# Diagonal state blocks in the ring of ScalarE's copied sums, one sigmoid and SyncE's branch hint placed elsewhere

## Chip, cores and metric

One core of a Trainium2 chip runs the whole program. The metric is the device time in microseconds (us), the median of three runs. The engines are named as the profile names them: PE (TensorE's matmuls, with PEld for its weight loads), DVE (VectorE), ACT (ScalarE), POOL (GpSimd) and SP (SyncE, which here only issues transfers). A "q" after the name (ACTq, SPq) means the engine's sequencer: it waits, branches or issues a DMA while the engine itself does nothing.

## What is computed

A gated linear recurrence runs over 768 steps for 4 batches and 8 heads of 48 channels, and its output goes through a SwiGLU block (384 to 1536 to 384), all in fp32:

```python
f = 1.0 / (1.0 + np.exp(-f_logit))
for t in range(S):
    state = f[:, :, t, :, None] * state + np.einsum('bhd,bhe->bhde', k[:, :, t], v[:, :, t])
    y[:, :, t] = np.einsum('bhd,bhde->bhe', q[:, :, t], state)
x = y.transpose(0, 2, 1, 3).reshape(B * S, H * D)
g = x @ w_gate
out = (g * (1.0 / (1.0 + np.exp(-g))) * (x @ w_val)) @ w_out
```

## The kernel before

**Chunks and stages.** The sequence is cut into six chunks (c = 0 to 5) of 128 steps. In a chunk each of the four batches (b = 0 to 3) is one unit of attention. `attention(u)` is a generator whose steps are laid by hand between other work: the sigmoid of the gates (L580 from the third chunk on), transposes and scans on DVE, scores on PE (L647), `decay` (the state times the chunk's decay), the outputs `y` (L683 to L708), and the new state (L737). When a chunk's attention is done, its 512 tokens go through the SwiGLU block while the next chunk's attention runs beside it. From the second chunk on, that block (`mlp_fifteen`) computes four groups of fifteen products (L988), whose results ScalarE copies out of PSUM or DVE combines, and then seven products of the down projection (`down_seven`, L1087 and L1150).

**The order.** `times(c)` gives each step of each batch a place on a time line, and `come_in` calls the steps due before each product. `in_order` then fixes each engine's order to the order in which the program was written. An instruction that waits on ACT therefore holds everything written after it on ACT.

**Outputs of the attention.** For b = 0 to 2 of a later chunk, `y` is copied by ScalarE into the tile `yT` (L691, tag `"x"`, one buffer in the pool `att`), and ten small DMAs carry it from there into `xT`, the input of the SwiGLU block. From the third chunk on POOL issues them (L698). For b = 3 no copy through `yT` is needed: the states are laid out as a block diagonal matrix, `diagonal`, so that PE writes `y` directly in the layout of `xT` (L708), and ScalarE copies it there (L723). `decay` builds `diagonal`: ScalarE fills it with zeros (L568) and copies the two halves of the decayed states in (L570). Its tile has the tag `"x"` too. It is the same single buffer as `yT`, so L568 waits until the ten DMAs of b = 2 have read it.

**ScalarE's copied sums.** `aside` (L997) copies a product out of PSUM into a ring of three tiles with the tag `"aside"` in the pool `comb` (128 x 512 fp32 each); DVE adds or subtracts it soon after. Each group of fifteen products uses the ring six times.

**The down projection's banks.** In `down_seven`, step `two` ends with ScalarE's copy of a product into the output tile (L1113, `ob`). That product lies in the one PSUM bank with the tag `"B"`, and step `four` (`o5`, the matmuls `o<-ws,hs`) takes the same bank.

**The chunk's end.** `put_out` (L1096) sends half of a chunk's outputs from ACT's queue and the other half from POOL's (SP's in the last chunk). The sigmoid of chunk 3, batch 1 is placed by the list `sigmoid` in `times` (L872), 4 units ahead of the end of chunk 1's block of products, which is on the time line the place ahead of `seven`.

**The branch.** A second, general program (`general_path`) follows, for gates too small for the short way. A flag decides: `judge` computes it in the last chunk, all five engines load it (L1355), get a branch hint (L1357, `mark_branch_hint_location("redo", 0, ...)`), and branch at L1361. With these inputs the general program is skipped, so each engine jumps to the end of its instruction stream. There SP waits for the transfers that are still out, and all engines meet.

**Completion semaphores.** SP's and ACT's transfers share eight completion semaphores, handed out in turn. A transfer that is given one waits until the transfer that had it before has landed.

## Time and profile before

| | us |
|---|---|
| three runs | 608.42, 608.66, 609.53 |
| median | 608.66 |
| the profiled execution, whole | 609.78 |
| its span, first to last instruction | 608.0 |
| granted TensorE clock in it | 0.999 |

| engine | busy us | share of the span | instructions |
|---|---|---|---|
| PE | 592.7 | 97% | 4028 |
| DVE | 476.9 | 78% | 825 |
| ACT | 292.7 | 48% | 557 |
| POOL | 70.1 | 12% | 175 |

The profile is one execution. What lies around its span (609.78 less 608.0, 1.8 us) is launch and finish. A line of a timeline or of the chain of waits gives start in us, duration in us, engine, operation, and in square brackets the idle time before it with what ended it. In a list of waits the three numbers are the sum, the count and the longest. In a list of operations of one line the three durations are least, median and greatest in ns, followed by the first and the last start. Matmuls are pipelined, so those of one group start closer together than they last: the 24 matmuls of a 128x192 half step take 3.9 us from the first start to the next group's start.

### The profile page before, as it was taken

The numbers are of one execution on the slowest core, as the hardware profiler recorded it, in microseconds if no ns is written. First come the engines' busy times: TensorE is split into PE (matmuls) and PEld (weight loads), VectorE is DVE, ScalarE is ACT, GpSimd is POOL, SyncE is SP. The second block draws the span as 40 slices with busy tenths as digits, with TensorE's granted clock in tenths as the row PEclk, the third lists the DMA queues.
The fourth block names the chain that finished last, engine by engine and source line by source line (L and its number), as shares of the span: only waits on it lengthen the run. The fifth ranks groups of instructions, "written<-read, shape, count | busy, mean of one in ns | idle before, by whom it ended". The sixth has DMA issues, their size and how long they took to land.

```text
span 608.0 us, 10812 instructions
## 1 busy us (share of the span) xinstructions
PE 592.7 (97%) x4028; PEld 487.8 (80%) x4028; DVE 476.9 (78%) x825; ACT 292.7 (48%) x557; POOL 70.1 (12%) x175
## 2 busy tenths in 40 slices
PE   7899999999999999999999999999999999999996
PEld 5744555667888899878899888898988899988896
DVE  7999885968999977988895978994878981666731
ACT  3567662314776512476622476732276731366600
POOL 1000000000030150030330030330030321000000
PEclk9999999999999999999999999999999999999999
DMA  9999461014331145333344333253241100100001
GB/s 202 236 246 357 140 196 27 8 33 130 79 92 48 37 113 129 93 96 96 77 111 122 91 101 95 62 135 85 74 105 52 28 8 8 53 1 1 1 1 56
DMA packets 110300, 55.12 MB, mean 91 GB/s; under 512 B 72992, under 2 KB 102688, under 8 KB 110240
## 3 DMA queue, kind: packets, MB, share of 16 engines
q1 hardware_dynamic: 103872, 47.67, 30.0%
q0 software_dynamic: 4352, 3.94, 2.0%
q10 hardware_dynamic: 2016, 2.75, 1.2%
q8 instruction: 33, 0.54, 0.4%
q14 instruction: 27, 0.22, 0.1%
HBM read 44.56 MB, written 6.82 MB: 85 GB/s over the span
## 4 chain that ended last, share of the span: by engine, by line
PE 84%; DVE 10%; DMA 2%; issue 1%; ACT 1%; POOL 1%; SPq 0%; ACTq 0%; DVEq 0%; POOLq 0%
PE o L1087 17%; PE A L988 15%; PE B L988 12%; PE gate L786 5%; PE val L786 5%; PE c L988 5%; PE o L988 5%; PE sc L647 4%; PE o L1150 3%; PE o L809 3%; PE y L708 2%; PE y L687 2%; PE dS L728 1%; PE y L683 1%; DVE c L892 1%
## 5 line engine op out<-in xcount | busy, mean ns | idle before, releaser
L698 POOL DMA_DIRECT2D xT<-yT x120 | 59.9, 507 | 53.8 <-ACT yT L691 52.2
L988 PE MATMUL A<-xs,w_both 128*128 128x256 f32 x240 | 62.3, 382 | 1.0 <-ACT c L993 1.0
L1087 PE MATMUL o<-w_out,h 128*128 128x192 f32 x360 | 62.0, 327 | 0.5 <-DVE h L940 0.5
L1087 PEld LDWEIGHTS o<-w_out,h 128*128 128x128 f32 x360 | 58.7, 190 | 1.7 <-DVE h L940 0.8
L993 ACT COPY c<-A 128x512 f32<-128x512 f32 x40 | 23.3, 582 | 58.9 <-PE A L988 48.9
L988 PEld LDWEIGHTS A<-xs,w_both 128*128 128x128 f32 x240 | 44.8, 190 | 7.9 <-ACT c L993 1.4
L993 ACT COPY aside<-A 128x512 f32<-128x512 f32 x60 | 35.0, 584 | 33.1 <-PE A L988 33.0
L889 DVE TENSOR_TENSOR c<-c,aside 128x512 f32<-128x512 f32 x60 | 41.1, 686 | 12.1 <-ACT aside L993 10.4
L940 DVE TENSOR_TENSOR h<-h,c 128x256 f32<-128x256 f32 x100 | 40.5, 414 | 7.8 <-ACT h L1004 7.6
L662 DVE TENSOR_TENSOR A<-sc,causal 128x512 f32<-128x512 f32 x48 | 30.9, 685 | 17.2 <-PE sc L647 17.1
L892 DVE TENSOR_TENSOR c<-c,aside 128x512 f32<-128x512 f32 x60 | 41.0, 683 | 2.5 <-ACT aside L993 2.5
L1004 ACT ACTIVATE h<-c 128x256 f32<-128x256 f32 x100 | 39.2, 416 | 7.8 <-DVE c L889 5.6
L1087 PE MATMUL o<-ws,h 128*128 128x192 f32 x240 | 41.5, 328 | 0.2 <-DVE A L662 0.2
L988 PE MATMUL B<-xs,w_both 128*128 128x256 f32 x160 | 41.3, 380 | 0.1
L988 PE MATMUL A<-xs,extra 128*128 128x256 f32 x160 | 41.3, 380 | 0.0
L988 PE MATMUL c<-xT,w_both 128*128 128x256 f32 x160 | 41.2, 380 | 0.1
L988 PE MATMUL B<-xT,extra 128*128 128x256 f32 x160 | 41.1, 379 | 0.0
L635 POOL MEMSET gates<- 128x4 f32 x24 | 2.9, 122 | 327.9 <-DVE qT L559 322.8
L993 ACT COPY aside<-B 128x512 f32<-128x512 f32 x60 | 35.1, 584 | 9.7 <-PE B L988 6.7
L1087 PEld LDWEIGHTS o<-ws,h 128*128 128x128 f32 x240 | 39.1, 190 | 0.8 <-DVE A L662 0.4
L889 DVE TENSOR_TENSOR c<-c,o 128x384 f32<-128x384 f32 x15 | 8.3, 552 | 36.8 <-PE o L1087 36.8
L892 DVE TENSOR_TENSOR c<-o,c 128x512 f32<-128x512 f32 x40 | 27.4, 684 | 10.6 <-ACT h L1004 6.2
(142 smaller groups left out, 1199.9 us busy)
## 6 DMA issues: line engine op xcount, KB each, us to landing
fsquares<-in_f_logit_dram SPq DMA_DIRECT2D x64, 96.0 KB, 2.5
qsquares<-in_q_dram SPq DMA_DIRECT2D x64, 96.0 KB, 2.2
ksquares<-in_k_dram SPq DMA_DIRECT2D x64, 96.0 KB, 2.3
v<-in_v_dram SPq DMA_DIRECT2D x24, 192.0 KB, 2.9
w<-in_moe_w_gate_dram SPq DMA_DIRECT2D x6, 768.0 KB, 6.5
w<-in_moe_w_val_dram SPq DMA_DIRECT2D x6, 768.0 KB, 5.4
w<-in_moe_w_out_dram SPq DMA_DIRECT2D x6, 768.0 KB, 4.6
out_dram<-ob ACTq DMA_DIRECT2D x14, 192.0 KB, 2.5
```

Of the source, the lines that this page charges most:

```text
L647: nc.tensor.matmul(sc[par][:, a * C:(a + 1) * C], lhsT=kT[r, a, :], rhs=qT[r, a, :], start=True, stop=True)
L662: nc.vector.tensor_tensor(A[:, par], sc[par].rearrange("p (a t) -> p a t", t=C), causal.unsqueeze(1).broadcast_to((128, HP, C)), ALU.mult)
L698: (nc.gpsimd if c >= SQUARES else nc.sync).dma_start(out=xT[c][f % 128:f % 128 + n, f // 128, b * C:(b + 1) * C], in_=yT[r:r + n, par, a / ...
L786: nc.tensor.matmul(p, lhsT=w[:, j, i, :], rhs=xT[c][:, i, :], start=(i == 0), stop=(i == KT - 1))
L809: nc.tensor.matmul(p, lhsT=hidden_tile(h, n // 2)[:, n % 2 * 2 + b // 2, b % 2 * C:(b % 2 + 1) * C], rhs=w_out[:, j, :], start=(n == 0), s ...
L889: nc.vector.tensor_tensor(dst, a, b, ALU.add)
L892: nc.vector.tensor_tensor(dst, a, b, ALU.subtract)
L940: lagging.append(lambda: f(*args))
L988: nc.tensor.matmul(p[name][:, n, :], lhsT=weights_of[a][:, n, j, :], rhs=tokens[b], start=fresh and n == 0, stop=True, skip_group_check=True)
L993: nc.scalar.copy(t, p[name])
L1004: nc.scalar.activation(dst, src[:, 0, :], AF.Silu)
L1087: nc.tensor.matmul(p[:, n, :], lhsT=lhsTs[j][:, n * C:(n + 1) * C], rhs=rhs[:, j, :], start=first and j == order[0] and n == 0, stop=j == ...
```

## The change

From the third chunk on (`c >= SQUARES`, which is 2) `diagonal` is taken from the ring `"aside"` in place of the buffer `"x"`; 384 of a ring tile's 512 values per partition are used. The second chunk (c = 1) keeps the buffer `"x"`. The sigmoid of chunk 3, batch 1 is placed at -1.5 in place of -4. SP gets its branch hint from a call placed before the steps of chunks 2 to 5 are written; the call in `judge` hints the other four engines only.

```diff
@@ decay, in attention
-                diagonal = att.tile([128, HP, 2 * D], FP32, tag="x", name="diagonal")
+                if c < SQUARES:
+                    diagonal = att.tile([128, HP, 2 * D], FP32, tag="x", name="diagonal")
+                else:
+                    room = comb.tile([128, 2, TH], FP32, tag="aside", name="diagonal", bufs=3)
+                    diagonal = room.rearrange("p n t -> p (n t)")[:, 0:HP * 2 * D].rearrange("p (a d) -> p a d", a=HP)
                 nc.scalar.copy(diagonal.rearrange("p a d -> p (a d)"), spare.broadcast_to((128, HP * 2 * D)))
@@ times
-        sigmoid = [-14 if c == 3 else SCORES[c - 1][-1][0] - whole - 0.01 if c > 3 else 0, -4 if c == 3 else at[0] - 0.01, *[t - 0.01 for t in at[1:]]]
+        sigmoid = [-14 if c == 3 else SCORES[c - 1][-1][0] - whole - 0.01 if c > 3 else 0, -1.5 if c == 3 else at[0] - 0.01, *[t - 0.01 for t in at[1:]]]
@@ short_path, before the steps of the later chunks
     mark = traced[-1]
+    tc.mark_branch_hint_location("redo", 0, [mybir.EngineType.SP])
     waiting = []
@@ judge
-        tc.mark_branch_hint_location("redo", 0, list(nc.engines))
+        tc.mark_branch_hint_location("redo", 0, [e for e in nc.engines if e != mybir.EngineType.SP])
```

In the built program PE, DVE and POOL keep their order. On ACT one place differs: at the end of chunk 1's block (in which chunk 2's attention runs) the two output DMAs (L1096) now stand ahead of the sigmoid of chunk 3, batch 1 with its table load and the small Silu that follows. On SP the hint is now the second instruction of the whole program, ahead of the first load. The waits differ in these places:

- The zero fill of `diagonal` (L568) no longer waits for the eight semaphores of POOL's DMAs in chunks 2 to 5.
- The first `yT` copy of chunks 3 to 5 (L691) now has that wait, for the DMAs of batch 2 one chunk earlier.
- The first copy into the ring after each `diagonal` waits for ScalarE's own earlier work.
- The completion semaphores of the transfers around the moved output DMAs are handed out differently: of the four loads of k for chunk 3, batch 1, the second now waits until the first output DMA has landed, and the fourth until the second has.

## The prediction

> **What bounds the kernel.** I read the page's shares of the critical chain first, then the waits of the whole run for the lines that the change touches, then the stage of each of those waits in the windows and the chain, and last the lines around the moved sigmoid and the branch. PE is busy 592.7 of 608.0 us, so an edit pays only where PE itself stops, or ahead of the first or behind the last matmul. First the chain's shares, then one line of the list of waits (sum, count, longest), then three lines of that list for the stage 396 to 424 us, where chunk 4's `diagonal` is built:

> ```profile
> PE 84%; DVE 10%; DMA 2%; issue 1%; ACT 1%; POOL 1%; SPq 0%; ACTq 0%; DVEq 0%; POOLq 0%
> ...
> ACT diagonal L568 <- DMA xT<-yT: 35.5, 5, 10.6
> ...
> ACT diagonal L568 <- DMA xT<-yT: 10.6, 1, 10.6
> PE o L1087 <- ACT ob L1113: 1.3, 1, 1.3
> DVE tails L631 <- ACT least L625: 0.9, 1, 0.9
> ```

> The zero fill costs ACT 35.5 us in five waits, but only one of them is seen to end in a wait of PE. The chain of the same stage (start, duration, instruction) shows the path:

> ```profile
> 408.66 6.01 DMA xT<-yT
> 414.92 0.52 ACT diagonal L568
> ...
> 416.20 0.49 ACT ob L1113
> 416.73 4.17 PE o L1087 x24
> ```

> POOL issues ten DMAs; ACT's zero fill waits until the last lands; the copy `ob`, written behind it, waits in the queue; PE's step `o5` waits for `ob` to free its PSUM bank. The step before began at 411.34, and such a step takes 3.90 us from start to next start, so PE wanted `o5` at 415.24 and began at 416.73: 1.49 us lost. The next lines are from the timeline, of chunk 3, where the same `ob` ran in time: it ended at 320.60, and `o5` began at 321.94 without waiting.

> ```profile
> 320.12 0.48 ACT L1113 COPY ob<-o 128x384 f32<-128x384 f32 x1
> 321.94 4.06 PE L1087 MATMUL o<-ws,hs 128*128 128x192 f32 x24
> ```

> Then the branch, from the list of operations of L1361 (durations in ns; first and last start):

> ```profile
> L1361 SPq EVENT_SEMAPHORE  x8: 17/17/17, 605.7 to 606.3; - x8
> L1361 POOLq COMPARE_BRANCH  x1: 68/68/68, 536.2 to 536.2; - x1
> L1361 POOLq EVENT_SEMAPHORE  x1: 17/17/17, 538.9 to 538.9; - x1
> L1361 ACTq COMPARE_BRANCH  x1: 68/68/68, 600.8 to 600.8; - x1
> L1361 ACTq EVENT_SEMAPHORE  x1: 17/17/17, 601.3 to 601.3; - x1
> ...
> L1361 SPq COMPARE_BRANCH  x1: 70/70/70, 603.0 to 603.0; - x1
> ```

> From branch to next instruction ACT needs 0.5 us, but SP and POOL 2.7. ACT's hint ran at 553.7, 47 us ahead. POOL's ran at 536.1, directly ahead of its branch, and did nothing. SP's ran at 536.1, 67 us ahead, and did nothing either. SP's eight waits at the branch's target then come 0.08 us apart, and the closing sequence of all engines begins behind the last of them.

> [...] in chunk 4 POOL's ten `yT` DMAs are issued at 404.19 to 409.17 while SP loads gates from 406.02 on, and take 6.4 us (median) and 7.0 (most) to land, where the page has medians of about 3. [...]

> **Part 1, the ring.** With `diagonal` in `"aside"` the zero fill waits for no DMA. Chunk by chunk, with the zero fill's wait from the trace of before:
> - Chunk 1 keeps the old buffer: its 7.2 us stay.
> - Chunk 2 (3.7 us, to 227.78): what is queued behind it on ACT is `least`, which at 229.07 itself waits for DVE, done at 228.95. Gain on PE: 0.
> - Chunk 3 (7.8 us, to 318.84): `ob` ended 1.3 us before PE needed it (above). Gain 0.
> - Chunk 4 (10.6 us, to 414.92): the fill could follow `decayed` (DVE, done at 407.9), and the product for `ob` is done at 411.44. `ob` then runs at about 411.5 to 412.0, 3.2 us before 415.24. The 1.49 us go; DVE's 0.9 us at `tails` was slack and counts nothing. What is late next is the matmul spacing itself.
> - Chunk 5 (6.2 us, to 504.53): `ob` ends at 506.29, `o5` starts at 508.81. Gain 0.

> The removed wait does not vanish: the first `yT` copy of chunks 3, 4 and 5 takes it. It asks for DMAs that landed at 227.7, 318.6 and 414.7, while those copies run at 261.6, about 351 and 446: over 30 us later, so only the instructions that test the semaphores remain, four extra at about 0.08 us, 0.3 us beside a table load and sigmoid of 1.9 us. The ring itself can cost where `diagonal` occupies one of three tiles: the next copies on the ring wait on work of ACT that is long done, and the zero fill gained no wait on DVE. I take 0, and 0.2 as the bad end. Part 1: -1.5, between -1.5 and 0. The zero end is kept because the profiled execution (609.78) is 1.1 us above the median, and part of this stall may be peculiar to it: the landing of ten contended DMAs decides it.

> **Part 2, the sigmoid of chunk 3, batch 1.** Before, from the timeline:

> ```profile
> 238.61 0.63 ACT L580 ACTIVATE fsquares<-fsquares 128x512 f32<-128x512 f32 x1 [3.31 <-DMA fsquares<-in_f_logit_dram]
> 239.17 0.35 ACTq L1096 DMA_DIRECT2D out_dram<-ob  x1
> 239.26 1.28 ACT L583 ACT_TABLE_LOAD   x1
> 239.56 0.47 ACTq L1096 DMA_DIRECT2D out_dram<-ob  x1
> 240.55 0.20 ACT L583 ACTIVATE spare<-spare 128x1 f32<-128x1 f32 x1
> 242.29 0.59 ACT L993 COPY c<-A 128x512 f32<-128x512 f32 x1 [1.54 <-PE A L988]
> ```

> The two output DMAs wait for DVE's `ob`, done at 239.14, so they stay at 239.17 to 240.03. Now the sigmoid comes behind them: 240.05 + 0.63 + 1.28 + 0.20 and small gaps ends at about 242.2. The copy `c` is wanted at 242.26, and DVE wants the gates at 243.6. The 1.5 us of slack is all but used: cost 0, up to 0.1. Were one issue as long as the longest on ACT's queue (1.37 us instead of 0.47), ACT's copy `c` would be 0.9 late, and PE at most as much behind it; that is the upper bound.

> The transfers issued beside it count too. Of chunk 3's k loads the second now waits for the first output DMA (landing about 242.25, as issued at 239.17 and with the page's 2.4 to 3.1 us) and the fourth for the second: issued to about 243.3 instead of 240.5, landing at about 245.6 to 246.4. DVE needs k at 247.45: 1.0 to 1.8 us of slack. SP's next loads (v, wanted at 256.3, and kt, at 257.2) come 3 us later with over 8 to spare. Cost 0.

> **Part 3, SP's hint.** It now stands second in SP's program, ahead of the first load. It lasts 60 ns; the first load starts at 0.81, its data is used by PE with 0.6 us to spare, the second load's with 0.1: cost 0 to 0.1. At the end, if a hint holds and SP needs 0.5 us like ACT, its eight waits begin at 603.5. The first seven are over by 604.1; the last asks for the last output DMA, which SP issued at 602.61 and which landed at 605.67. The closing sequence then starts at about 605.75 instead of 606.32: -0.55. The transfer is what is late next, so 0.55 and not 2.2 is the most that this can give. If it does not hold: 0. The trace speaks both ways. The hints of ACT and DVE, 47 and 50 us ahead, worked (0.5 and 0.6 us from branch to next instruction); SP's at 67 us ahead did not, so distance alone may spoil a hint, and 600 us is farther. On the other side SP's old hint stood directly in front of a 64 us wait, in which nothing was executed, so that its place and not its age may be at fault. I take it as working, by a little.

> **The sum.** Against the profiled execution: -1.5 (ring) - 0.55 (hint) + 0.1 (start and ACT's place) = -1.95, so 607.8 for 609.78. The same difference on the median of 608.66 gives 606.7.

> **The rivals.**
> - A, forecast: both gains come, 606.7 (chance 0.50; own range 606.3 to 607.3).
> - B, the hint at the start has no effect, and SP again spends 2.7 us: 608.66 - 1.5 + 0.05 = 607.2 (0.25). For it: the old hint, which also failed. Against: SP runs straight on from hint to branch[...].
> - C, the ring frees nothing in a timed run, because there the stall was short (landing of 5 instead of 6 us gives `ob` in time), or because `o5` meets another wait, such as the one on `xT` or DVE's `c`: 608.66 - 0.55 = 608.1, or up to 608.7 with B (0.17). For it: the profiled run is the slowest of all seen, and chunk 3 and 5 show the same wait without loss. Against: in the profile the wait of `o5` names `ob` and nothing else, and chunk 4's loads of SP are fixed in the program.
> - D, slower (0.08): [...] the first loads come 2.2 us late; PE's slack there is 0.6 for the first and 0.1 for the second, so about 2.1 on the start. With part 1's 1.5 taken off, +0.6: 609.3; without the gain of part 1, +2.1: 610.8. It decides from a delay of 1.6 us on, and exceeds the bound below from 2.8 on, or with C. For it: the hint's new place, with nothing to hide behind. Against: the hint lasts 60 ns, and at 536 SP's next instruction began 0.1 us after its hint.

> **How the numbers follow.** Measurements of this kernel tell about 0.2% apart, 1.2 us: faster is below 607.44, slower above 609.88. Faster: A nearly whole (0.47) and three quarters of B (0.19), 0.66. Slower: half of D, and a little from C with the copies late, 0.06. Same: the rest, 0.28. The range: from 606.1 (both gains, with 0.6 more from timed runs in which the landing was later) to 608.4, which takes in B and the better part of C; left out are D, the rest of C and an end below, under 2 in 10.

> **What would show it.** Right: no wait of L568 for xT<-yT from chunk 2 on, `o5` of chunk 4 following 3.9 us on the step before, no `o L1087 <- ACT ob` wait in that stage; ACT's `c` after the moved sigmoid not later than 0.1 behind its product; from SP's branch to its next instruction 0.5 us, and the closing sequence released by the last landing. Wrong: 2.7 us again behind the branch (B); a new wait in front of `o5` at about 415 (C); the first matmul 2 us later (D); DVE waiting for k at 247.

## The result, and the profile after

| | before | changed |
|---|---|---|
| median | 609.25 us (16 runs) | 607.30 us (16 runs) |
| lowest, highest | 608.42, 610.58 | 607.02, 608.63 |
| profiled execution, whole | 609.78 | 607.02 |
| its span | 608.0 | 605.3 |

The ratio is 0.9968 (95% interval 0.996 to 0.9975): 1.95 us, 0.32%, faster, as forecast (a difference of 1.95). In absolute time the forecast was 606.7 us, worked out from a median before of 608.66, which 16 runs put at 609.25. The 607.30 us alone lies nearer to rival B's 607.2, so what tells the two apart is the traces below. From L568 on, line numbers are four or five higher in the changed kernel: L568 is L572 there, L570 is L574, L1087 is L1091, L1113 is L1117, L1361 is L1366.

First the shares of the critical chain on the page of the changed kernel, then one line of its list of waits for the whole run (sum, count, longest):

```profile
PE 87%; DVE 9%; issue 1%; ACT 1%; DMA 1%; SPq 0%; DVEq 0%; ACTq 0%
```

```profile
ACT diagonal L572 <- DMA xT<-yT: 7.2, 1, 7.2
```

PE's share of the chain rises from 84 to 87%, and DMA's falls from 2 to 1%. Of the five waits of the zero fill only chunk 1's is left, 7.2 of 35.5 us. The stage that carried the first part of the forecast, 396 to 424 us, in the list of waits:

```profile
ACT diagonal L574 <- DVE decayed L564: 3.6, 1, 3.6
ACT ob L1117 <- PE o L1091: 2.5, 1, 2.5
```

The zero fill no longer waits here. ScalarE's copy of the states into `diagonal`, behind the fill, now waits for VectorE's `decayed`, and `ob` waits for its own product; no line of PE waiting for `ob` is left. The timeline of the changed kernel around it (start, duration, operation, and the idle time before it):

```profile
411.06 4.06 PE L1091 MATMUL o<-ws,h 128*128 128x192 f32 x24
411.26 0.48 ACT L1117 COPY ob<-o 128x384 f32<-128x384 f32 x1 [2.51 <-PE o L1091]
...
414.96 4.06 PE L1091 MATMUL o<-ws,hs 128*128 128x192 f32 x24
```

`ob` runs beside the half step before, and `o5` follows it after 414.96 - 411.06 = 3.90 us, the plain spacing. In the chain of waits of this stage POOL, DMA and ScalarE are gone; PE alone is left, in one piece of 84 matmuls around `o5`:

```profile
405.18 13.85 PE o L1091 x84
```

The moved sigmoid, on ScalarE's timeline, is within about 0.1 us of where the sum put it; its group ends at 242.3 us where the forecast had 242.2:

```profile
239.15 0.82 ACTq L1100 DMA_DIRECT2D out_dram<-ob  x2
240.16 0.63 ACT L584 ACTIVATE fsquares<-fsquares 128x512 f32<-128x512 f32 x1 [4.88 <-DMA ksquares<-in_k_dram]
240.80 1.28 ACT L587 ACT_TABLE_LOAD   x1
242.10 0.20 ACT L587 ACTIVATE spare<-spare 128x1 f32<-128x1 f32 x1
242.28 0.59 ACT L997 COPY c<-A 128x512 f32<-128x512 f32 x1
```

The copy `c` starts at 242.28 (before: 242.29). The bracket of the second line is one of those to be read with care: ScalarE was idle as an engine, but its sequencer was issuing the two output transfers until just before.

The branch, from the list of operations of L1366 (durations in ns, first and last start in us):

```profile
L1366 SPq EVENT_SEMAPHORE  x8: 17/17/17, 601.6 to 603.6; - x8
...
L1366 SPq COMPARE_BRANCH  x1: 70/70/70, 601.1 to 601.1; - x1
```

SP needs 0.5 us from branch to next instruction, not 2.7. Its eight waits, which stood 0.08 us apart, are now spread over 2.0 us: the last of them ends at 603.6, with the landing of the last output transfer (603.57).

The two profiled executions are 2.66 us apart in span, more than the medians are. Laid side by side by the starts of the same matmuls: 0.07 us at the start, 0.22 at 262.5, 1.47 at `o5`, 0.14 at 435.8, and from SP's branch to the end 0.77, of which 0.20 is a quicker landing of the last transfer (2.86 us from issue in place of 3.06). The medians are the better measure of the change, and the experiments show why.

### The profile page after: what moved, and what is told of

Read it like the earlier page. It is cut to its first block, busy times and chain, and to the rows that moved or that the text cites. A ratio compares the mean times of both kernels' runs of the same rounds, so it can differ in the third digit from the quotient of the medians.

```text
span 605.3 us, 10815 instructions
## 1 busy us (share of the span) xinstructions
PE 592.4 (98%) x4028; PEld 487.7 (81%) x4028; DVE 476.5 (79%) x825; ACT 292.5 (48%) x557; POOL 70.4 (12%) x175
## 3 DMA queue, kind: packets, MB, share of 16 engines
q0 software_dynamic: 4352, 3.94, 1.9%
## 4 chain that ended last, share of the span: by engine, by line
PE 87%; DVE 9%; issue 1%; ACT 1%; DMA 1%; SPq 0%; DVEq 0%; ACTq 0%
PE o L1091 19%; PE A L992 15%; PE B L992 12%; PE gate L790 5%; PE val L790 5%; PE c L992 5%; PE o L992 5%; PE sc L651 4%; PE o L1154 3%; PE o L813 3%; PE y L691 2%; PE y L712 2%; PE dS L732 2%; PE y L687 1%; DVE c L896 1%
## 5 line engine op out<-in xcount | busy, mean ns | idle before, releaser
L1091 PE MATMUL o<-w_out,h 128*128 128x192 f32 x360 | 62.0, 327 | 0.5 <-DVE h L944 0.5
L1091 PEld LDWEIGHTS o<-w_out,h 128*128 128x128 f32 x360 | 58.7, 190 | 1.7 <-DVE h L944 0.8
L1091 PE MATMUL o<-ws,h 128*128 128x192 f32 x240 | 41.5, 328 | 0.2 <-DVE A L666 0.2
L1091 PEld LDWEIGHTS o<-ws,h 128*128 128x128 f32 x240 | 39.1, 190 | 0.8 <-DVE A L666 0.4
L896 DVE TENSOR_TENSOR c<-o,c 128x512 f32<-128x512 f32 x40 | 27.3, 684 | 10.6 <-ACT h L1008 6.2
```

What stands on the lines that cost most here:

```text
L896: nc.vector.tensor_tensor(dst, a, b, ALU.subtract)
L1091: nc.tensor.matmul(p[:, n, :], lhsT=lhsTs[j][:, n * C:(n + 1) * C], rhs=rhs[:, j, :], start=first and j == order[0] and n == 0, stop=j == ...
```

## The experiments

**Each part alone.** Three kernels take one part of the diff each, a fourth takes the ring in one chunk. All four ran on one chip, beside 67 runs of the kernel before (median 609.10).

The ring alone is the first hunk of the diff as it stands.

> The kernel before with the first part of the change alone (diagonal in the ring from the third chunk on). My reading: the chunk 4 step o5 no longer waits for ScalarE's copy ob, 1.5 us of the span go, and 0.1 to 0.3 more may go at 262.5 us, where in the changed kernel PE waits 0.76 us for ScalarE's copy instead of 1.03. So about 1.5 to 1.8 us under the kernel before, ratio 0.997 to 0.9975. Rival (the stall is peculiar to one execution, or another wait takes its place): under 0.5 us, ratio above 0.999, with a new wait of PE near 415 us in the trace.

Measured: 608.07 us, ratio 0.9982 (0.9973 to 0.9991), 1.1 us less. No wait of PE for `ob` is left in its trace, and nothing took its place. The mechanism is as I read it; the gain is less than the 1.5 to 1.8 us that I expected, though its interval (0.5 to 1.6 us) reaches into that range.

The ring in chunk 4 alone:

```diff
-                diagonal = att.tile([128, HP, 2 * D], FP32, tag="x", name="diagonal")
+                if c != 4:
+                    diagonal = att.tile([128, HP, 2 * D], FP32, tag="x", name="diagonal")
+                else:
+                    room = comb.tile([128, 2, TH], FP32, tag="aside", name="diagonal", bufs=3)
...
```

> The kernel before with diagonal in the ring in chunk 4 only; chunks 1, 2, 3 and 5 keep the buffer that yT uses, with their waits of ScalarE (7.2, 3.7, 7.8 and 6.2 us). My reading: those waits have slack behind them, so this is as fast as the ring from the third chunk on, 1.5 us under the kernel before, within 0.3 us of that run. Rival (the other chunks' waits also cost, only hidden in one profile): it gains clearly less, 0.5 to 1 us.

Measured: 608.31 us, ratio 0.9986 (0.9979 to 0.9994), 0.8 us less (0.4 to 1.3). The 1.5 us that I expected did not come. What the run is for, the difference to the ring from the third chunk on, is 0.24 us, within the 0.3 that I expected. The intervals overlap widely, so a small gain in the other chunks isn't excluded, but the bulk is chunk 4's.

The hint alone is the third and fourth hunk of the diff.

> The kernel before with SP's branch hint moved to the front of its program, and nothing else. My reading: 0.5 us instead of 2.7 us from SP's branch to its next instruction; the closing sequence is then released by the landing of the last output transfer, so 0.55 to 0.75 us less, ratio 0.9988 to 0.9991; the chunk 4 stall stays at 1.5 us. Rival (the early hint delays SP's first loads): PE's first matmuls later by up to 2 us and the kernel slower. Second rival (the hint worked only together with the rest): 2.7 us stay, ratio 1.000.

Measured: 608.15 us, ratio 0.9985 (0.9978 to 0.9992), 0.9 us less (0.5 to 1.3), where I had expected 0.55 to 0.75. Branch to next instruction took 0.5 us, and from SP's branch to the end of the span it is 3.94 us, before 4.95. The first transposes of the inputs start at 4.21 us as before, so the early hint costs the start nothing. This run also keeps the old `diagonal`. I had expected its stall to stay at 1.5 us; its timeline, and one line of the chain of waits, show that the stall varies:

```profile
412.88 4.06 PE L1087 MATMUL o<-ws,h 128*128 128x192 f32 x24
417.64 4.17 PE L1087 MATMUL o<-ws,hs 128*128 128x192 f32 x24 [0.69 <-ACT ob L1113]
```

```profile
410.21 5.37 DMA xT<-yT
```

417.64 - 412.88 - 3.90 = 0.86 us lost, where the profiled execution of before lost 1.49.

The sigmoid alone is the second hunk (-4 to -1.5).

> The kernel before with the sigmoid of chunk 3, batch 1 placed at -1.5, and nothing else. My reading: no time, ratio 0.9995 to 1.0005: the copy c behind the sigmoid starts at most 0.1 us after its product, and k lands 1 us or more before VectorE wants it. Rival: the 0.2 us that went at 262.5 us come from this part (the loads stand differently), ratio 0.9996 with the wait of PE there at 0.76 us; or the later k loads stop VectorE at 247 us and it is slower, 1.001 to 1.003.

Measured: 608.98 us, ratio 0.9994 (0.9986 to 1.0003): no difference that can be told from none. `c` starts at 242.43, right behind the sigmoid's group, and VectorE doesn't wait for k at 247. PE's wait for `c` at 262.5 us, of which the expectations for this run and for the ring alone speak, is 0.74 us here and 0.75 with the ring alone (1.03 before). But two traces of the changed kernel itself have 0.76 and 1.26, so it differs between executions, and neither part can be credited with it. This third trace with the old `diagonal` has the smallest stall at `o5`:

```profile
411.19 4.06 PE L1087 MATMUL o<-ws,h 128*128 128x192 f32 x24
415.66 4.17 PE L1087 MATMUL o<-ws,hs 128*128 128x192 f32 x24 [0.41 <-ACT ob L1113]
```

415.66 - 411.19 - 3.90 = 0.57 us. The chain of waits of this stage has the reason: the last of POOL's transfers took 6.01 us in the profiled execution of before, 5.37 in the hint's run and 5.09 here. In all three it is issued 2.67 or 2.68 us ahead of the step before `o5`, and the stall is its time less 4.51 or 4.52 us: in these three the landing alone sets the stall.

```profile
408.51 5.09 DMA xT<-yT
413.85 0.52 ACT diagonal L568
...
415.66 4.17 PE o L1087 x24
```

The mean of the three stalls is (1.49 + 0.86 + 0.57) / 3 = 0.97 us, between what the ring's two timed runs gave (1.1 and 0.8), though three executions are few. The first profile had shown the largest of the three.

**Where SP's hint works.** The old hint had failed (2.7 us), and distance, the place in front of a long wait, or something else could be to blame. The reading under test is one of place alone: that the hint has to stand ahead of the last transfer before the branch that I take for SP's in the profile's instruction queue q14, at 365.99 us in the trace of before and at 354.50 us in that of the changed kernel (the expectations call it the theory of the next block). Four kernels move it through SP's program, by one more entry in the list of timed steps (130, 170, 195.5 and 259 for some 300, 345, 375 and 450 us). Each was executed once; the single times (607.56, 607.68, 608.10 and 608.17 us in this order, 608.88 for the kernel before) fit, but it is the traces that are read here:

```diff
-    tc.mark_branch_hint_location("redo", 0, [mybir.EngineType.SP])
...
+    waiting.append((195.5, lambda: tc.mark_branch_hint_location("redo", 0, [mybir.EngineType.SP])))
     waiting.sort(key=lambda x: x[0])
```

> The changed kernel with SP's hint in the middle of its program, at about 300 us. In the traces SP's instruction stream seems to be fetched in blocks, the last crossing ahead of the branch at about 355 to 366 us; the hint at 536 us stood behind it and had no effect. Theory [...]: 0.5 us from SP's branch to its next instruction. Rival (age or the first place in the program is what counts): 2.7 us.

> As the one at 300 us, with SP's hint at about 345 us, still ahead of the last crossing. Theory of the next block: 0.5 us behind the branch. Rival (the old hint failed because a 64 us wait followed it directly): also 0.5, so this one is the near side of the pair with the next.

> As before, with SP's hint at about 375 us, behind the last crossing, with some 90 instructions of SP between hint and branch and no long wait directly behind it. Theory of the next block: 2.7 us behind the branch, the closing sequence some 0.6 us later than in the changed kernel. Rival (the long wait behind the old hint was at fault): 0.5 us.

> As before, with SP's hint at about 450 us, behind the last crossing and 150 us ahead of the branch. Theory of the next block: 2.7 us. Rival (enough time or enough instructions between hint and branch): 0.5 us.

From the two inner ones, the list of operations of the branch's line; first the hint at about 345 us, then the one at about 375:

```profile
L1366 SPq EVENT_SEMAPHORE  x8: 17/17/17, 602.2 to 604.2; - x8
...
L1366 SPq COMPARE_BRANCH  x1: 70/70/70, 601.7 to 601.7; - x1
```

```profile
L1366 SPq EVENT_SEMAPHORE  x8: 17/17/17, 604.0 to 604.6; - x8
...
L1366 SPq COMPARE_BRANCH  x1: 70/70/70, 601.2 to 601.2; - x1
```

0.5 us in the one, 2.8 in the other: 20 us and 22 instructions of SP lie between them, and between them lies a transfer of the instruction queue, at 355.2 us in the first of the two. Of the two readings in my forecast, age is out: the hints that fail (from 373.3 us on) are the younger ones. A wait behind the hint isn't out yet: against what I expected, SP runs nothing for 8.5 us (373.4 to 381.9) right behind the hint at 373.3. Nor do the two tell the transfer from a least distance to the branch, since the one hint stands 103 instructions ahead and the other 81. One more kernel, executed once too (607.25 us), keeps the distance and what follows the hint and moves the hint against these transfers, with 70 drains (instructions that compute nothing) ahead of the hint:

```diff
+    waiting.append((100, lambda: [nc.sync.drain(fusable=False) for _ in range(70)]))
     waiting.append((195.5, lambda: tc.mark_branch_hint_location("redo", 0, [mybir.EngineType.SP])))
```

The same list for this kernel:

```profile
L1367 SPq EVENT_SEMAPHORE  x8: 17/17/17, 602.1 to 603.8; - x8
...
L1367 SPq COMPARE_BRANCH  x1: 70/70/70, 601.6 to 601.6; - x1
```

0.5 us again, with the hint still 81 instructions ahead and the same 8.5 us wait behind it (373.7 to 382.3): neither the distance nor the wait decides. The instruction queue now shows transfers at SP's 336th instruction (283.2 us) and at its 467th (422.6 us, behind the hint at 373.6). Side by side, counted in the instructions of the engine itself, the last two rows for POOL (whose transfers weren't told apart):

```
hint, us   instructions   transfer taken as SP's,      branch to next
           to branch      between hint and branch      instruction, us
536.1        5            none                         2.7   (before)
446.0       22            none                         2.7
373.3       81            none                         2.8
373.6       81            422.6                        0.5   (70 drains)
352.8      103            355.2                        0.5
300.7      160            at about 355                 0.5
  0.8      432            three times                  0.5   (changed)
536.1        1            -                            2.7   (POOL, before)
  0.8      239            -                            0.5   (POOL, below)
```

Which engine a transfer of the instruction queue belongs to isn't written in the trace. In that of before, transfers of 8 KB start at 72.93, 234.24 and 365.99 us, when SP has begun its 81st, 209th and 337th instruction; in that of the changed kernel at 71.90, 233.54 and 354.50 us, at the 81st, 209th and 336th. That these are SP's, one for about 128 instructions, is my estimate from their places, and from the drains having moved them.

ScalarE's and VectorE's hints agree. They worked (0.5 and 0.6 us from branch to next instruction) from 52 and 62 instructions ahead of their branches, nearer than the 81 at which SP's failed. In the trace of before two transfers of the instruction queue start at 580.2 us, between these hints (553.7 and 552.1) and their branches (600.8 and 602.2), while SP and POOL execute nothing. SP's branch fits too: behind it the six traces in which its hint fails have three transfers of 8 KB in that queue, the eight in which it works have two. So in these traces a transfer taken as SP's between its hint and branch goes with 0.5 us, and none with 2.7 or 2.8; why it does isn't shown.

**POOL too.** Its hint stood directly ahead of its branch. Here it goes to the front of POOL's program with SP's:

```diff
-    tc.mark_branch_hint_location("redo", 0, [mybir.EngineType.SP])
+    tc.mark_branch_hint_location("redo", 0, [mybir.EngineType.SP, mybir.EngineType.Pool])
```

> The changed kernel with POOL's branch hint at the front of its program too. Theory [...]: POOL's next instruction comes 0.5 us behind its branch instead of 2.7 us, and the time stays as it is within 0.5 us, since POOL has nothing left to do at that point. Rival (the early place works for SP alone): 2.7 us stay.

```profile
L1366 POOLq COMPARE_BRANCH  x1: 68/68/68, 534.5 to 534.5; - x1
L1366 POOLq EVENT_SEMAPHORE  x1: 17/17/17, 535.0 to 535.0; - x1
```

0.5 us in place of 2.7 (the list of operations of the branch's line), and 607.14 us in one execution, inside the changed kernel's spread: 2.2 us saved on an engine that nobody waits for.

**A version that beats both.** Every trace with the old order of loads has one more stop of PE, at 262.5 to 264.3 us, of 0.90 to 1.49 us. The changed kernel's line:

```profile
262.46 1.13 PE L992 MATMUL A<-xs,w_both 128*128 128x256 f32 x4 [0.76 <-ACT c L997]
```

`c` stands behind a sigmoid whose gates land late, because their load is issued at 255.2 us only, though VectorE has emptied their buffer by 244.7. This kernel loads them as soon as that is done, and only q and k at the old place:

```diff
             nc.vector.transpose(in_turn(pairs(gate)[:, :, 1:N1]), squares("f"))
+            if u + 1 < len(units):
+                load(u + 1, "f")
...
-            load(w, "fkqv" if units[w][1] < SQUARES or w == SQUARES * B else "fkq")
+            load(w, "fkqv" if units[w][1] < SQUARES or w == SQUARES * B else "kq")
```

> The changed kernel once more, beside the next run and on the same chip. If the parts add (ring -1.0, sigmoid -0.1 to 0, hint -0.9, as measured alone): ratio 0.9968, within 0.0005. If the ring and the hint shared a gain: 0.9975 or above.

> The changed kernel with the gates of the next batch loaded as soon as VectorE has turned the present ones, instead of a step group later. In every trace so far PE stops 0.9 to 1.5 us at about 262.5 us, because ScalarE's copy c stands behind the sigmoid of chunk 3, batch 2, which waits for its gates to land. Theory (that landing is the cause): ScalarE's wait for fsquares there goes, PE's stop falls to under 0.3 us, and 0.8 to 1.3 us go, ratio 0.9947 to 0.9955 against the kernel before. Rival (SP's queue is only held by the new load's own wait, and q, k or the scores come late instead): no gain or up to 1 us slower than the changed kernel.

Measured beside each other, with the kernel before at 609.13: the changed kernel again 607.10, ratio 0.9966 (0.9954 to 0.9978), as the sum of the parts had it; with early gates 605.73, ratio 0.9946 (0.9932 to 0.9960), 1.4 us less than the changed kernel (0.8 to 1.3 expected). Its timelines, ScalarE's, then PE's:

```profile
255.74 1.28 ACT L584 ACT_TABLE_LOAD   x1
257.03 0.63 ACT L584 ACTIVATE fsquares<-fsquares 128x512 f32<-128x512 f32 x1
```

```profile
260.63 1.03 PE L994 MATMUL o<-xT,w_both 128*128 128x256 f32 x4
261.49 1.03 PE L994 MATMUL A<-xs,w_both 128*128 128x256 f32 x4
```

The table load starts with no wait, 3.7 us earlier than in the changed kernel (259.46), and PE's products follow each other after 0.86 us.

## Why the prediction was right, point by point

- **What bounds the kernel.** Right. PE's stops were what could be won, and the five waits of the zero fill cost only where `o5` stood behind one: 28.3 of the 35.5 us that ScalarE waited for `yT`'s transfers went, and about 1 us of time.
- **Part 1, the ring.** Mechanism and place right, size too large: -1.5 was this one execution's stall; alone it is 1.1 us (0.5 to 1.6), in chunk 4 alone 0.8 (0.4 to 1.3). The sum carried a quantity that hangs on the landing of POOL's last transfer (6.01, 5.37 and 5.09 us in three traces) as if it were fixed. The bounds (-1.5 to 0), and the note that the profiled execution lay above the median, were the right warning; the mean of several profiles would have been the right term. The waits that the `yT` copies took over cost nothing that shows.
- **Part 2, the sigmoid.** Right: 0.9994 (0.9986 to 1.0003) alone, with `c` at 242.28 where I had the group end at about 242.2.
- **Part 3, the hint.** It works, and the start costs nothing. The term "0.55 and not 2.2 is the most that this can give" failed as a bound. The 0.9 us of the hint alone (0.5 to 1.3) would still allow 0.55; the traces don't. From SP's branch to the end of the span the six traces in which SP's hint fails have 4.95 to 5.09 us, whatever the last landing. The eight in which it works have 3.94 to 4.64, each of them the landing of the last output transfer plus 1.3 us. The working took that landing as fixed at 3.06 us, which is the second longest of the fourteen traces: they have 2.46 to 3.32, mean 2.81. With 4.98 us as the mean of the six and 1.32 of the eight less their landings, the hint frees 4.98 - 1.32 = 3.66 us less the landing: 0.3 to 1.2, and 0.85 at the mean. That the transfer is what is late next was right.
- **The two errors cancel**: 1.5 + 0.55 forecast, 1.1 + 0.9 measured alone. The hit on 1.95 us is partly luck.
- **The rivals.** B (no effect of the hint) fell: 0.5 us. For its doubt, my two reasons, age and the long wait, were both beside the point. Of C the half about a smaller stall holds, with 0.57 to 1.49 us rather than nothing; a wait in its place did not come. D (slower, by first loads that come 2.2 us late) fell: the first transposes start at 4.20 or 4.21 us in every trace.

## What to carry to other kernels

On SP the hints at 0.8 to 352.8 us and, with the drains, at 373.6 us worked, each with a transfer taken as SP's between hint and branch; those at 373.3, 446.0 and 536.1 us, with none, didn't. At the front of the program a hint worked for SP and for POOL, at no cost that shows; from branch to next instruction (0.5 us, or 2.7 to 2.8) the profile says whether it did. A long wait of a side engine is worth what the next stop of the bounding engine behind it is worth (here 28.3 us of waits and about 1 us of time), and where that wait ends with a transfer's landing, its price is a spread (here 0.57 to 1.49 us): read it in several executions before it goes into a sum. The same goes for a saving that ends at a landing (2.46 to 3.32 us from issue, in fourteen traces).

## What the runs showed that I had not expected

- The place of SP's hint decided all or nothing: 22 instructions and 20 us apart, one saves 2.2 us of SP (0.5 us from branch to next instruction) and the other nothing (2.8). Why isn't shown.
- Executions differ by stops in few places: 0.57 to 1.49 us at `o5` in three traces with the old `diagonal`, and at 262.5 us 0.92 and 1.42 in two traces of the changed kernel itself. In the hint's run PE also stopped 1.2 us at 77.6 us, for VectorE's `qT`, a stop that the profile of before doesn't have, nor any of the four other traces with SP's hint in front. Between 28 and 40 us VectorE had waited 1.2 us there for a load of the weights `w_gate`, which it doesn't in the trace of before. Whether the one stop comes from the other wasn't tried.
